# An early zero store to the output tensor, issued by ScalarE among the first loads, in a one-core decode kernel

## The chip, the core and the metric

The kernel runs on one core of a Trainium2 chip. The time is device time in microseconds of one execution. The profile is one further look at one execution; its span is about 1.8 us shorter than the timed figure, and times in views count from the start of the span.

Engines are named as in the profile: PE is the matrix engine (PEld its weight loads), DVE the vector engine, ACT ScalarE, POOL GpSimd and SP SyncE. A "q" after the name (ACTq, SPq) means an instruction handled by the engine's sequencer, such as the issue of a DMA. An issue only starts a transfer; the data land later. A completion semaphore is a counter that a DMA raises when its data have landed, so that others can wait for it.

## The reference, cut to what matters

```
g = sigmoid((x * gate_w).sum(-1))
a = attention(x @ wq, k_cache, v_cache) @ wo      # 32 heads, 4 KV heads, 65,536 keys, head size 128
b = gated MLP of x (w_in, layer norm, w_sp, b_sp, w_out)
return g * a + (1 - g) * b                        # 1 x 1 x 1024, bf16: 2 KB
```

One token is decoded. K and V are 67 MB each, the weights some 28 MB, all bf16, and all of it is read once. The result is 2 KB, so everything about the output is tiny beside the reads.

## The kernel before

The parts that matter are the first loads, the pool of four 32 KB-per-partition buffers that holds every big load, and the tail.

```python
# first loads: four small ones from ScalarE, four big ones from SyncE
nc.scalar.dma_start(out=xg8[:, 0, :], in_=A_x.rearrange(...))       # 8 rows x 256 B
nc.scalar.dma_start(out=xg8[:, 1, :], in_=gate_w.rearrange(...))
nc.scalar.dma_start(out=wb[:, 0:1], in_=B_w_sp)                     # one element
nc.scalar.dma_start(out=wb[:, 1:2], in_=B_b_sp.unsqueeze(0))        # one element
win_t = [load(win_view[:, i * KH:(i + 1) * KH, :], (KH, F), "win_t") for i in range(2)]   # SyncE
wq_t = [load(wq_view[:, i * KH:(i + 1) * KH, :], (KH, HD), "wq_t") for i in range(2)]
# ... constants by GpSimd and DVE, MLP, query; then 32 loads of K and V of 4 MB each ...
# tail: the last weights come in pieces of 16, 8, 4, 2, 1, 1 (4096 KB down to 256 KB)
for split in WO_SPLIT:
    # ... nc.sync.dma_start of a piece, then project() it into out_ps ...
out_sb = const.tile([P, NO], BF16, name="out_sb")
nc.scalar.copy(out=out_sb[:], in_=out_ps[:])
nc.scalar.dma_start(out=out.rearrange("o t (q n) -> (o t q) n", n=NO), in_=out_sb[::B, :])
```

The build puts in the semaphores. Each DMA gets one of eight completion semaphores, in turn, over all DMAs of SyncE and ScalarE together. A DMA that comes round to a semaphore waits until that semaphore's earlier DMA has landed.

Of the kernel before, what the change touches and what calls it, by code (L numbers as in the profile page):

```python
# [8 lines left out]
BF16 = mybir.dt.bfloat16  # L9
# [5 lines left out]
P = 128  # L15
CT = 128
NKV = 4
B = 32
NB = P // B
# [8 lines left out]
def kernel(  # L28
# [15 lines left out]
    nc = tc.nc  # L44

    _, _, D = A_x.shape
# [19 lines left out]
    const = ctx.enter_context(tc.tile_pool(name="const", bufs=1))  # L66
# [43 lines left out]
    def load_kv(src, g, j, name):  # L110
# [8 lines left out]
    wb = const.tile([1, 2], BF16, name="wb")  # L119
    nc.scalar.dma_start(out=wb[:, 0:1], in_=B_w_sp)  # L120
    nc.scalar.dma_start(out=wb[:, 1:2], in_=B_b_sp.unsqueeze(0))

    KH = KC // 2
    win_view = B_w_in.rearrange("(p c) n -> p c n", c=KC)
# [10 lines left out]
    erow = const.tile([KC, KC, P // KC], FP32, name="erow")  # L135
    nc.gpsimd.iota(erow[:], pattern=[[1, KC], [0, P // KC]], base=0, channel_multiplier=0,
                   allow_small_or_imprecise_dtypes=True)
    ones_f = const.tile([P, P], FP32, name="ones_f")
    nc.gpsimd.memset(ones_f[:], 1.0)
    wt = [big.tile([P, VC, BP, NB, VC, REP], BF16, name=f"wt{i}") for i in range(2)]  # L140
# [31 lines left out]
    for t in range(2):  # L172
        nc.vector.tensor_tensor(
            out=xm[:, t], in0=xb_ps[:, t * P:(t + 1) * P].rearrange("p (i c) -> p c i", c=KC),
# [51 lines left out]
    for hf in range(2):  # L226
        nc.vector.tensor_tensor(  # L227
            out=zm[:, hf], in0=z_ps[:, hf * HN:hf * HN + ZN].rearrange("p (j c) -> p j c", c=FC),
# [3 lines left out]
                            in_=zm.rearrange("p h j c -> p h c j"), axis=AX.X, op=ALU.add)  # L232
# [44 lines left out]
    for k in range(NHB):  # L277
        xs = slice(k * NX // NHB, (k + 1) * NX // NHB)
        nc.vector.tensor_tensor(  # L279
            out=qm[:, xs], in0=q_ps[:, k * HN:(k + 1) * HN].rearrange("p (x j e) -> p x j e",  # L280
                                                                   j=B, e=2),
# [6 lines left out]
        out=q4[:], in0=q1[:].rearrange("p x e -> p (x e)").unsqueeze(1).to_broadcast(  # L288
            [P, NB, NX * 2]),
# [7 lines left out]
    for g in range(G):  # L297
        k, t0 = g * T2 // NB, g * T2 % NB
        nc.vector.tensor_copy(out=qs[:, g].rearrange("p b (t h) -> p b t h", t=T2),
                              in_=qv[:, k, t0:t0 + T2].rearrange("p t h b -> p b t h"))  # L300
# [107 lines left out]
    NO = D // NB  # L408
# [35 lines left out]
    for split in WO_SPLIT:  # L444
        t = kv.tile([P, CT * P], BF16, name="wo_t", tag="kv")
        t = t[:].rearrange("p (c n) -> p c n", n=D)
        b = c0
        for n in split:
            nc.sync.dma_start(out=t[:, c0 - b:c0 - b + n, :], in_=wo_view[:, c0:c0 + n, :])  # L449
            project(t[:, c0 - b:c0 - b + n, :], n, oa, c0, last=(c0 + n == OC))  # L450
            c0 += n
    out_sb = const.tile([P, NO], BF16, name="out_sb")
    nc.scalar.copy(out=out_sb[:], in_=out_ps[:])  # L453
    nc.scalar.dma_start(out=out.rearrange("o t (q n) -> (o t q) n", n=NO), in_=out_sb[::B, :])

    last = {}
    for ins in list(nc.cur_bb.bb.instructions):
# [36 lines left out]
```

## Time and profile before

Three runs before the prediction: 385.80, 385.75 and 385.86 us.

| | before |
|---|---|
| DMA queue of SyncE | 98.5% of 16 engines' span, 422 GB/s |
| PE, DVE, ACT busy | 63%, 57%, 10% |
| first big packets (packet records) | 1.74 us |
| last weights landed | 380.64 us |
| end of the span | 383.92 us |

The first view below is the page: its DMA row in 40 slices of 9.6 us (tenths of busy time), the queue of SyncE, and the chain of waits by engine.

```profile
DMA  8999999999999999999999999999999999999995
q1 hardware_dynamic: 6192, 162.01, 98.5%
DMA 60%; DVE 20%; PE 11%; issue 5%; ACT 2%; SPq 1%; DVEq 0%; ACTq 0%
```

The stream of loads is full from the second slice on. DVE's and PE's shares of the chain lie beside it.

The timeline (start, duration, engine, line and operation) at the start of the kernel before:

```profile
0.74 0.61 ACTq L117 DMA_DIRECT2D xg<-in_A_x_dram  x1
1.39 0.29 ACTq L118 DMA_DIRECT2D xg<-in_gate_w_dram  x1
2.00 0.27 ACTq L121 DMA_DIRECT2D wb<-in_B_b_sp_dram  x1
2.31 1.28 ACT L190 ACT_TABLE_LOAD   x1 [2.31 <-issue]
7.64 0.37 PE L169 MATMUL xb_ps<-xg,spread 8*128 8x256 bf16 x1 [7.64 <-DMA xg<-in_gate_w_dram]
...
15.54 0.33 SPq L107 DMA_DIRECT2D kn<-in_A_k_cache_dram  x1
```

The first issue on ScalarE took 0.61 us, the three after it 0.27 to 0.29. The end of the chain of waits, and then the timeline of the last store:

```profile
349.05 31.60 DMA wo_t<-in_A_wo_dram
...
380.69 0.32 PE out_ps L414 x4
```

```profile
381.02 0.37 ACT L453 CAST out_sb<-out_ps 128x256 bf16<-128x256 f32 x1 [47.61 <-PE out_ps L414]
381.43 0.61 ACTq L454 DMA_DIRECT2D out_dram<-out_sb  x1
```

### The profile page before, as it was taken

What the parts mean: (1) busy time and instruction counts of PE and PEld (TensorE: products, weight loads), DVE (VectorE), ACT (ScalarE), POOL (GpSimd) and SP (SyncE); (2) the same over time, 40 slices, a digit from 0 to 9 for tenths busy, and PEclk for the clock granted to TensorE, in tenths of its full rate; (3) what the DMA queues carried; (4) which work ended last, traced back from release to release, by engine and by line L of the source; (5) the groups of instructions that cost most, each with busy time, mean ns of one, the idle gap of its engine ahead of it and who ended that gap; (6) DMA issues with size and microseconds to landing.
All of it is one profiled execution on the core that took longest, in us unless ns stands there. A gap on an engine that the chain in (4) does not pass through costs nothing.

```text
span 383.9 us, 2650 instructions
## 1 busy us (share of the span) xinstructions
PE 242.3 (63%) x1372; PEld 59.3 (15%) x796; DVE 218.5 (57%) x211; ACT 39.6 (10%) x55; POOL 4.4 (1%) x10
## 2 busy tenths in 40 slices
PE   0433447976449948466699393774993937685553
PEld 0110001111202201011121020121220201121122
DVE  5141478988497563658975545679754546730040
ACT  1010001100511101014011010140110101400000
POOL 4000000000000000000000000000000000000000
PEclk9996559889659989686599797865997869888868
DMA  8999999999999999999999999999999999999995
GB/s 335 430 437 437 435 434 430 423 431 426 428 427 437 435 430 437 427 434 430 423 432 427 437 437 422 430 434 437 427 425 427 437 438 427 425 430 431 434 411 203
DMA packets 6248, 162.18 MB, mean 422 GB/s; under 512 B 728, under 2 KB 732, under 8 KB 1116
## 3 DMA queue, kind: packets, MB, share of 16 engines
q1 hardware_dynamic: 6192, 162.01, 98.5%
q8 instruction: 8, 0.13, 0.1%
q14 instruction: 4, 0.03, 0.0%
q10 hardware_dynamic: 44, 0.01, 0.0%
HBM read 162.01 MB, written 0.00 MB: 422 GB/s over the span
## 4 chain that ended last, share of the span: by engine, by line
DMA 60%; DVE 20%; PE 11%; issue 5%; ACT 2%; SPq 1%; DVEq 0%; ACTq 0%
DMA kn<-in_A_k_cache_dram 47%; DVE kt L320 16%; DMA wo_t<-in_A_wo_dram 8%; PE s_ps L326 8%; DMA win_t<-in_B_w_in_dram 5%; DVE pt L362 2%; PE o_ps L372 2%; ACT sc L337 1%; PE z_ps L213 1%; ACT sc L359 1%; DVE mx L341 1%; DVE o_sb L387 0%; SPq L449 0%; ACT L359 0%; PE nb_ps L352 0%
## 5 line engine op out<-in xcount | busy, mean ns | idle before, releaser
L326 PE MATMUL s_ps<-kt,wt 128*128 128x512 bf16 x512 | 142.3, 437 | 67.9 <-DVE kt L320 67.3
L320 DVE STREAM_TRANSPOSE kt<-kn 128x2048 int32<-128x2048 int32 x64 | 143.3, 2284 | 63.5 <-DMA kn<-in_A_k_cache_dram 63.4
L372 PE MATMUL o_ps<-vt,pt 128*64 128x512 bf16 x512 | 69.2, 432 | 8.8 <-DMA vt<-in_A_v_cache_dram 8.8
L326 PEld LDWEIGHTS <-wt 128*128 128x128 bf16 x256 | 27.6, 108 | 184.0 <-issue 122.9
L337 ACT CAST sc<-s_ps 128x1024 bf16<-128x1024 f32 x16 | 16.2, 1013 | 253.8 <-PE s_ps L326 253.8
L372 PEld LDWEIGHTS <-pt 128*64 128x64 bf16 x256 | 17.2, 124 | 57.9 <-issue 56.4
L362 DVE STREAM_TRANSPOSE pt<-sc 128x1024 bf16<-128x1024 bf16 x16 | 18.6, 1218 | 6.8 <-ACT sc L359 6.8
L383 DVE TENSOR_TENSOR om<-o_ps,own 128x1024 f32<-128x1024 f32 x4 | 4.8, 1205 | 26.8 <-PE o_ps L372 26.8
L359 ACT ACTIVATE sc<-sc,nb 128x1024 bf16<-128x1024 bf16 x16 | 18.2, 1139 | 10.2 <-DVE nb L355 10.2
L322 DVE TENSOR_REDUCE mx<-sc 128x1 f32<-128x1024 bf16 x12 | 14.3, 1192 | 4.4 <-ACT sc L337 4.4
L341 DVE TENSOR_REDUCE mx<-sc 128x1 f32<-128x1024 bf16 x4 | 4.9, 1220 | 12.3 <-ACT sc L337 12.3
L213 PE MATMUL q_ps<-wq_t,xT 128*32 128x512 bf16 x64 | 7.2, 630 | 7.3 <-DMA wq_t<-in_A_wq_dram 7.3
L393 PE MATMUL om_ps<-o_sb,hsel 128*32 128x128 f32 x8 | 2.4, 398 | 13.6 <-DVE o_sb L387 13.6
L213 PE MATMUL z_ps<-win_t,xT 128*32 128x448 bf16 x64 | 6.4, 577 | 4.9 <-DMA win_t<-in_B_w_in_dram 4.9
L414 PE MATMUL out_ps<-wo_t,oa 128*32 128x256 bf16 x128 | 6.3, 346 | 4.6 <-DMA wo_t<-in_A_wo_dram 3.2
L279 DVE TENSOR_TENSOR rowt<-q_ps,own_b 128x512 f32<-128x512 f32 x2 | 1.3, 686 | 12.4 <-PE q_ps L213 12.4
L345 PE MATMUL mt_ps<-ident_f,m 128*1 128x128 f32 x4 | 1.4, 346 | 10.2 <-DVE m L343 10.2
L387 DVE TENSOR_REDUCE o_sb<-om 128x128 f32<-128x1024 f32 x4 | 7.5, 1871 | 0.1
L227 DVE TENSOR_TENSOR rowt<-z_ps,own_b 128x448 f32<-128x448 f32 x2 | 1.2, 620 | 9.6 <-PE z_ps L213 9.6
L213 PEld LDWEIGHTS <-xT 128*32 128x32 bf16 x64 | 3.0, 140 | 20.3 <-issue 20.3
L453 ACT CAST out_sb<-out_ps 128x256 bf16<-128x256 f32 x1 | 0.4, 372 | 47.6 <-PE out_ps L414 47.6
L414 PEld LDWEIGHTS <-oa 128*32 128x32 bf16 x128 | 4.2, 119 | 6.9 <-issue 4.2
(88 smaller groups left out, 57.9 us busy)
## 6 DMA issues: line engine op xcount, KB each, us to landing
kn<-in_A_k_cache_dram SPq DMA_DIRECT2D x16, 4096.0 KB, 26.5
vt<-in_A_v_cache_dram SPq DMA_DIRECT2D x16, 4096.0 KB, 32.9
wq_t<-in_A_wq_dram SPq DMA_DIRECT2D x2, 4096.0 KB, 28.4
win_t<-in_B_w_in_dram SPq DMA_DIRECT2D x2, 3584.0 KB, 15.1
wo_t<-in_A_wo_dram SPq DMA_DIRECT2D x1, 4096.0 KB, 27.2
wout_t<-in_B_w_out_dram SPq DMA_DIRECT2D x1, 3584.0 KB
wo_t<-in_A_wo_dram SPq DMA_DIRECT2D x1, 2048.0 KB
wo_t<-in_A_wo_dram SPq DMA_DIRECT2D x1, 1024.0 KB
```

The costliest lines, as they stand in the source:

```text
L213: ins = nc.tensor.matmul(ps[t * B:(t + 1) * B, k * HN:k * HN + n], lhsT=xT[:, i * KH + c:i * KH + c + 1].to_broadcast([P, B]), rhs=w[:, c, ...
L320: nc.vector.transpose(out=kt[:].bitcast(I32), in_=kb[:, v * n:(v + 1) * n])
L322: nc.vector.reduce_max(**late.pop())
L326: ins = nc.tensor.matmul(s_ps[:, k * HN:(k + 1) * HN], lhsT=wt[g % 2][:, v, b].rearrange("p a v h -> p (a v h)"), rhs=kx[:, b // 2, b % 2, ...
L337: nc.scalar.copy(out=sct[g, j][:], in_=s_ps[:])
L341: nc.vector.reduce_max(**late.pop())
L359: nc.scalar.activation(out=sct[g, j][:], in_=sct[g, j][:], func=ACT.Exp, scale=SCALE, bias=nb[:, 0:1], accum_out=lss[g][:, j:j + 1])
L362: nc.vector.transpose(out=ptt[g, j][:].rearrange("p c x -> p (c x)"), in_=sct[g, j][:])
L372: ins = nc.tensor.matmul(o_ps[g][hs, e, :], lhsT=ptt[g, j][:, 2 * u:2 * u + 2, :].rearrange("p c x -> p (c x)"), rhs=vx[:, 2 * u + e], sta ...
L383: nc.vector.tensor_tensor(out=om8[:], in0=o_ps[g][:].rearrange("p e (v d) -> p (e v) d", d=DH), in1=own_8[:].unsqueeze(2).to_broadcast([P, ...
L387: nc.vector.tensor_reduce(out=o_sb[:], in_=om8[:].rearrange("p x d -> p d x"), axis=AX.X, op=ALU.add)
L414: nc.tensor.matmul(out_ps[t * B:(t + 1) * B, :], lhsT=vec[:, c0 + c:c0 + c + 1].to_broadcast([P, B]), rhs=w[:, c, t * NO:(t + 1) * NO], st ...
```

## The change

The zero store touches the output once, early. It can have been meant to take some first-use cost of the output path (an address entry, a cold write) away from the exposed last store. The result is overwritten at the end, so the kernel stays correct.

```diff
     nc.scalar.dma_start(out=wb[:, 1:2], in_=B_b_sp.unsqueeze(0))
+    out_view = out.rearrange("o t (q n) -> (o t q) n", q=NB)
+    out_sb = const.tile([P, D // NB], BF16, name="out_sb")
 ...
+    nc.gpsimd.memset(out_sb[:], 0.0)
+    nc.scalar.dma_start(out=out_view, in_=out_sb[::B, :])
     ones_f = const.tile([P, P], FP32, name="ones_f")
     nc.gpsimd.memset(ones_f[:], 1.0)
 ...
-    out_sb = const.tile([P, NO], BF16, name="out_sb")
     nc.scalar.copy(out=out_sb[:], in_=out_ps[:])
-    nc.scalar.dma_start(out=out.rearrange("o t (q n) -> (o t q) n", n=NO), in_=out_sb[::B, :])
+    nc.scalar.dma_start(out=out_view, in_=out_sb[::B, :])
```

## The prediction

> **What bounds the kernel.** The stream of loads. The DMA table gives the SyncE queue 98.5% of 16 engines' span, 422 GB/s for 162 MB; in the 40 slices DMA stands at 9 tenths in all but the first and last. No compute engine is over 63%. The chain that ended last is 60% DMA, and its DVE and PE pieces lie beside a full DMA queue. So a small change counts only at the start, if it starved the load queue, and in the tail after the last load.
>
> **What the change adds.**
> 1. A GpSimd memset of 128x256 bf16 ahead of two others. The 128x128 f32 memset beside it took 0.20 us, so the GpSimd work behind it and the DVE setup held up beside that (two instructions of 3.3 us, to 5.1 us) move by about 0.2 us. PE's first matmul waits for the small ScalarE loads until 7.6 us: hidden.
> 2. A fifth ScalarE DMA, after four loads (issued 0.74 to 2.27 us, taking 0.61, 0.29, 0.27, 0.27). The table load behind it slips by 0.3 to 0.6 us; it ended at 3.6, and ScalarE's first work is at 12.4: hidden. Its four 512-byte rows stand behind the loads on the ScalarE rings, so they delay none. The Trainium skill (DMA: Bandwidth & Descriptors, "Queues, rings and completion order") says a DMA engine takes queues in turn by packets; the packet records agree: the last small loads come 1.1 us apart between 28 KB packets. The zeros should land at 12 to 14 us (estimate); nobody waits for them.
> 3. The last copy and last store must follow the zero store, done 370 us before: at most one more satisfied wait, 0.02 to 0.05 us by such waits in the trace.
>
> 2 KB written against 162 MB read is nothing. Even 1 us lost at the start is free: the four big loads already queued hold the DMA engines for about 35 us (15.7 MB at 430 GB/s, estimate), and the next is queued at 15.5.
>
> **What it could remove.** Only the tail is exposed: last weights land 380.64, copy 381.02 to 381.39, store issued 381.43 to 382.04, its packets 383.13 to 383.23, closing barrier to 383.9. If the aim is to warm the output's path, its reach is small: the packets take 0.1 us, so no slow first write is to be saved. The issue took 0.61 us, as did ScalarE's first DMA, against 0.27 to 0.29 for the next three. If the extra 0.33 us belongs to a first use of the output (its address entry, the store direction), the early store pays it and the end saves 0.3 us. If it is the price of a ScalarE queue that has not issued for a while, nothing is saved. I hold the second likelier (2 in 3): each later load was the first use of its own tensor, at 0.27 to 0.29. The 1.1 us from issue to packets should stay; SyncE's loads show the same.
>
> **Sum.** Minus 0.3 us with one chance in three, otherwise zero to plus 0.05: 385.7 us. Three runs before lie within 0.11 us.
>
> **What would show each step.** The early store's issue at 2.3 us, 0.6 long in the first theory, 0.3 in the second; the last issue 0.3 or 0.6. First matmul still at 7.6, first K load queued at 15.5, mean 422 GB/s, last weights landing at 380.6. HBM written 4096 bytes instead of 2048.
>
> **What would make it wrong.** A store among the loads that slows the stream by more than its bytes; a shifted memory layout; completion semaphores, handed round among DMAs, making a load wait for another transfer than before; a tail changed by something in the barrier that the profile doesn't name.

## More of the kernel before

The order of the first DMAs, read from the built programs (the zero store marked *):

```
semaphore        0     1       2        3      4      5       6       7       0 (waits)   1 (waits)
before           A_x   win[0]  gate_w   w_sp   b_sp   win[1]  wq[0]   wq[1]   K 0         K 1
changed          A_x   win[0]  gate_w   w_sp   b_sp   store*  win[1]  wq[0]   wq[1]       K 0
```

The trace's packet records put the four 512-byte packets of the last store, with their completion writes, at 382.67 to 382.77 us. SyncE's closing wait for them goes on at 383.11.

## The result

| | median, us | runs | range |
|---|---|---|---|
| before | 385.77 | 4 | 385.62 to 385.86 |
| changed | 385.87 | 4 | 385.68 to 385.88 |

The ratio is 1.0002, with a 95% interval of 0.9984 to 1.0019. Ratios here are the mean time of one kernel's fast runs over that of the other's of the same rounds, so not quite the ratio of the medians. The time is the same.

The page of the changed kernel, the same three rows:

```profile
DMA  8999999999999999999999999999999999999994
q1 hardware_dynamic: 6192, 162.01, 98.4%
DMA 67%; DVE 20%; issue 6%; PE 5%; ACT 1%; SPq 1%; DVEq 0%; ACTq 0%
```

The stream is as full as before. (The chain's 60 and 67% differ in its middle, where DVE and PE work lies beside a full queue; both chains begin and end alike.) The start of the changed kernel, in its timeline:

```profile
1.31 0.30 POOL L140 MEMSET out_sb<- 128x256 bf16 x1
2.01 0.27 ACTq L121 DMA_DIRECT2D wb<-in_B_b_sp_dram  x1
2.32 0.61 ACTq L141 DMA_DIRECT2D out_dram<-out_sb  x1
2.96 1.28 ACT L194 ACT_TABLE_LOAD   x1 [2.96 <-issue]
7.68 0.37 PE L173 MATMUL xb_ps<-xg,spread 8*128 8x256 bf16 x1 [7.68 <-DMA xg<-in_gate_w_dram]
...
15.38 0.33 SPq L107 DMA_DIRECT2D kn<-in_A_k_cache_dram  x1
```

The early store's issue took 0.61 us, directly behind an issue of 0.27. The table load slipped by 0.65 us. The first matmul moved from 7.64 to 7.68, and the first K load is queued at 15.38, 0.16 us earlier than before. The end of the chain and the last store:

```profile
349.88 30.78 DMA wo_t<-in_A_wo_dram
...
380.69 0.43 PE out_ps L418 x4
```

```profile
381.15 0.37 ACT L456 CAST out_sb<-out_ps 128x256 bf16<-128x256 f32 x1 [47.93 <-PE out_ps L418]
381.55 0.55 ACTq L457 DMA_DIRECT2D out_dram<-out_sb  x1
```

The last weights landed at 380.65, as before. The last issue took 0.55 us, not 0.61, and not 0.3. So neither of the two readings of the 0.61 us in the prediction fits: a first use would have given 0.61 and 0.3, an idle queue 0.3 and 0.61. That was the first thing to settle. The second came from the view of what SyncE's queue waited for (total us, times, longest), which has a line in the changed kernel that it did not have before:

```profile
SPq L107 <- DMA xg<-in_A_x_dram: 0.3, 1, 0.3
```

The fourth big load now waits for A_x, because the zero store moved every later DMA on by one completion semaphore (the table above). It waits 0.3 us, with three big loads queued, and nothing comes of it. The prediction had named this as a way to be wrong; the experiments ask how near it was.

### The profile page after: what moved, and what is told of

It reads as the page before. It is cut to its first block, busy times and chain, and to the rows that moved or that the text cites. A ratio compares the mean times of both kernels' runs of the same rounds, so it can differ in the third digit from the quotient of the medians.

```text
span 384.1 us, 2653 instructions
## 1 busy us (share of the span) xinstructions
PE 235.3 (61%) x1372; PEld 58.0 (15%) x796; DVE 218.6 (57%) x211; ACT 39.6 (10%) x55; POOL 4.6 (1%) x11
## 4 chain that ended last, share of the span: by engine, by line
DMA 67%; DVE 20%; issue 6%; PE 5%; ACT 1%; SPq 1%; DVEq 0%; ACTq 0%
DMA kn<-in_A_k_cache_dram 54%; DVE kt L324 17%; DMA wo_t<-in_A_wo_dram 8%; DMA win_t<-in_B_w_in_dram 5%; PE o_ps L376 2%; PE s_ps L330 1%; DVE pt L366 1%; PE z_ps L217 1%; ACT sc L341 1%; DVE o_sb L391 0%; SPq L453 0%; DVE mx L345 0%; DVE om L387 0%; DVE mx L326 0%; PE om_ps L397 0%
## 5 line engine op out<-in xcount | busy, mean ns | idle before, releaser
L330 PE MATMUL s_ps<-kt,wt 128*128 128x512 bf16 x512 | 136.1, 419 | 75.6 <-DVE kt L324 75.5
L330 PEld LDWEIGHTS <-wt 128*128 128x128 bf16 x256 | 26.7, 104 | 186.1 <-issue 121.2
L366 DVE STREAM_TRANSPOSE pt<-sc 128x1024 bf16<-128x1024 bf16 x16 | 18.6, 1217 | 6.8 <-ACT sc L363 6.8
L345 DVE TENSOR_REDUCE mx<-sc 128x1 f32<-128x1024 bf16 x4 | 4.9, 1220 | 12.1 <-ACT sc L341 12.1
L283 DVE TENSOR_TENSOR rowt<-q_ps,own_b 128x512 f32<-128x512 f32 x2 | 1.3, 686 | 12.1 <-PE q_ps L217 12.1
```

Of the source, the lines that this page charges most:

```text
L330: ins = nc.tensor.matmul(s_ps[:, k * HN:(k + 1) * HN], lhsT=wt[g % 2][:, v, b].rearrange("p a v h -> p (a v h)"), rhs=kx[:, b // 2, b % 2, ...
L345: nc.vector.reduce_max(**late.pop())
L366: nc.vector.transpose(out=ptt[g, j][:].rearrange("p c x -> p (c x)"), in_=sct[g, j][:])
```

## The experiments

Eleven kernels ran; all gave the reference's result. Times are medians, with the kernel before beside them.

| run | us | before | ratio, 95% interval |
|---|---|---|---|
| e1_probe | 386.05 (1 run) | 385.76 | |
| e2_late_store | 385.75 (1 run) | 385.76 | |
| e3_late_load | 385.81 (1 run) | 385.76 | |
| e4_sync_store | 385.70 | 385.76 | 0.9997 (0.9983 to 1.0011) |
| e5_slow_start | 385.95 | 385.82 | 1.0002 (0.9986 to 1.0019) |
| e6_two_last | 387.51 | 385.82 | 1.0043 (1.0028 to 1.0058) |
| e7_four_early | 388.58 | 385.84 | 1.0073 (1.0060 to 1.0085) |
| e8_four_later | 386.09 | 385.84 | 1.0006 (0.9994 to 1.0019) |
| e9_after_again | 385.88 | 385.84 | 1.0001 (0.9987 to 1.0014) |
| e10_three_early | 385.95 | 385.79 | 1.0004 (0.9990 to 1.0018) |
| e11_one_fewer | 385.72 | 385.81 | 0.9996 (0.9982 to 1.0010) |

### What does the issue of a store cost? (e1 to e4)

The theory after the result: every store issue is dear, about twice a load's, whatever went before it. Rivals: a change between loads and stores costs, the first use costs, the shape costs, or an idle queue costs.

```diff
# e1_probe, on the changed kernel (gate_w is also loaded before A_x); h is 64 columns, 128 B
-    nc.scalar.dma_start(out=out_view, in_=out_sb[::B, :])
+    nc.scalar.dma_start(out=bx[:, 0, :], in_=bx_view)                          # L1
+    nc.scalar.dma_start(out=out_view[:, 0:h], in_=out_sb[::B, 0:h])            # S1
+    nc.scalar.dma_start(out=out_view[:, h:2 * h], in_=out_sb[::B, h:2 * h])    # S2
+    nc.scalar.dma_start(out=bx[:, 1, :], in_=bx_view)                          # L2
+    nc.scalar.dma_start(out=bx[:, 2, :], in_=bx_view)                          # L3
+    nc.scalar.dma_start(out=out_view[:, 2 * h:], in_=out_sb[::B, 2 * h:])      # S3
```

> In place of the one early zero store, ScalarE issues in this order: gate_w load, A_x load (swapped), two 1-element loads, load of 4 rows x 512 B of B_x (L1), store of 4 rows x 128 B (S1), another such store (S2), the B_x load twice (L2, L3), a store of 4 rows x 256 B (S3); the last store of the result stays. Issue times by theory. Store price (every ScalarE store costs about 0.6): L1, L2, L3 about 0.28, S1, S2, S3 all about 0.6, last store 0.55 to 0.61. Switch (a change between loads and stores, or an address window that has to move, costs): S1 0.6, S2 0.28, L2 0.6, L3 0.28, S3 0.6. First use of the output: S1 0.6, S2 and S3 0.28. Shape (4 rows of 512 B cost more than 8 of 256 B): L1, L2, L3 0.6 too. First issue on the queue: gate_w, now first, 0.61 and A_x 0.28; if A_x itself was dear, the reverse. Time: 385.8 within 0.3, all of it hidden, by every theory.

The timeline of e1_probe, its issues on ScalarE:

```profile
0.74 0.61 ACTq L117 DMA_DIRECT2D xg<-in_gate_w_dram  x1
1.39 0.29 ACTq L118 DMA_DIRECT2D xg<-in_A_x_dram  x1
...
2.41 0.26 ACTq L144 DMA_DIRECT2D bx<-in_B_x_dram  x1
2.71 0.59 ACTq L145 DMA_DIRECT2D out_dram<-out_sb  x1
3.34 0.52 ACTq L146 DMA_DIRECT2D out_dram<-out_sb  x1
3.90 0.47 ACTq L147 DMA_DIRECT2D bx<-in_B_x_dram  x1
11.95 0.25 ACTq L148 DMA_DIRECT2D bx<-in_B_x_dram  x1
12.24 0.54 ACTq L149 DMA_DIRECT2D out_dram<-out_sb  x1
```

The stores took 0.59, 0.52 and 0.54 us; loads of four rows of 512 B took 0.26 and 0.25. That is the store price. It rules out the number and length of the rows as the cause, and a switch as the cause of what a store costs: S2 follows a store and would have cost 0.28. One load does not fit: L2, directly behind two stores, took 0.47, where the store price said 0.28 and the switch 0.6. It is the only load right behind a store in any run, so a switch may still cost a load some 0.2 us. Why is open. gate_w, now first on the queue, took 0.61 and A_x behind it 0.29, so ScalarE's first issue is dear, whichever tensor it is for.

e1_probe's time, 386.05 in its one run, lies within the expected 0.3 of 385.8, and the runs of the kernel before reach 386.03. In its profile the last weights landed at 380.92 instead of 380.64. With six extra early DMAs the second big load waits for a small one until about 9.5 us, and the other two for others until 11.75 us. These waits led to e7, but that they cost e1_probe its 0.28 us is not shown: the rates of its stretches are 344 GB/s from 8 to 10 us (373 before) and 418 or more after that, and by 30 us both kernels had moved the same 12.1 MB.

```diff
# e2_late_store, on the kernel before: a store of a scratch tile late in the program
+    nc.scalar.copy(out=late_sb[:, :OC], in_=oa[:])        # waits for the last head, about 372 us
+    nc.scalar.dma_start(out=out.rearrange("o t (q n) -> (o t q) n", n=NO), in_=late_sb[::B, :])
# e3_late_load: the same copy, then a load instead
+    nc.scalar.dma_start(out=bx[:], in_=B_x.rearrange("o t (q n) -> (o t q) n", n=NO))
```

> The kernel before, with a store to the output issued by ScalarE at about 371.5 us (its source waits for the last head's result), some 10 us before the last store overwrites it. Recent use of the queue, or recent use of the output: the last store's issue falls to about 0.3 and the span by 0.3. Store price: the last issue stays at 0.55 to 0.61, span and time as before (385.8 within 0.3). Packets of the late store start some 1 to 3 us after its issue, among the loads of wo, which should land no later than 380.6 plus 0.1.

> As the late store, but a load of 4 rows x 512 B of B_x issued by ScalarE at about 371.5 us. Recent use of the queue: last store's issue falls to 0.3. Recent use of the output alone, or store price: stays 0.55 to 0.61. The late load's own issue, after 370 us without one on ScalarE, tells what a queue out of use costs for a load: 0.28 if idleness costs nothing, 0.6 if it does.

The timelines of e2_late_store and then of e3_late_load, near the end:

```profile
372.61 0.60 ACTq L443 DMA_DIRECT2D out_dram<-late_sb  x1
...
381.45 0.52 ACTq L458 DMA_DIRECT2D out_dram<-out_sb  x1
```

```profile
372.36 0.26 ACTq L444 DMA_DIRECT2D bx<-in_B_x_dram  x1
...
381.41 0.61 ACTq L459 DMA_DIRECT2D out_dram<-out_sb  x1
```

A load after some 370 us without an issue cost 0.26: an idle queue costs nothing, against what the prediction thought likelier. Using the queue 9 us earlier with a load left the last store at 0.61. Using it with a store brought it to 0.52.

```diff
# e4_sync_store, on the kernel before
-    nc.scalar.dma_start(out=out.rearrange("o t (q n) -> (o t q) n", n=NO), in_=out_sb[::B, :])
+    nc.sync.dma_start(out=out.rearrange("o t (q n) -> (o t q) n", n=NO), in_=out_sb[::B, :])
```

> The kernel before, with the one last store issued by SyncE instead of ScalarE; SyncE's isolated load issues took 0.33. If the price is ScalarE's own: issue 0.33 instead of 0.6 plus one semaphore hop of 0.02 to 0.05, span and time 0.2 to 0.25 lower, 385.55. If it is the price of any store: issue about 0.6 on SyncE too, time the same within 0.1.

The last store of e4_sync_store in its timeline:

```profile
381.52 0.65 SPq L454 DMA_DIRECT2D out_dram<-out_sb  x1
```

SyncE's loads of K are issued in 0.33; its store took 0.65. The price belongs to stores, not to ScalarE. One rival was left untested: every store here reads four partitions that lie 32 apart (`[::B, :]`), while every small load writes partitions side by side. No run stores from neighbouring partitions, so the direction and this stride are not separated. Over all profiles, the first store of a program took 0.59 to 0.65 us (before, changed, e1, e2, e3, e4) and every later one that stands alone in a timeline 0.52 to 0.55 (changed, e1, e2, e5 to e11). So the early store does save something at the end: 0.06 us.

### Is the start hidden and the tail exposed? (e5, e6)

```diff
# e5_slow_start, on the changed kernel
-    for t in wt:
+    for t in wt * 3:
         nc.gpsimd.memset(t[:], 0.0)
# e6_two_last, on the changed kernel: the last line twice, the second waits for the first
     nc.scalar.dma_start(out=out_view, in_=out_sb[::B, :])
+    nc.scalar.dma_start(out=out_view, in_=out_sb[::B, :])
```

> The changed kernel with the two GpSimd clears of wt done three times: 4 more memsets of about 1.8 us, so GpSimd ends its setup some 7 us later and the DVE instructions beside it too. Hidden start (my claim): first matmul at about 12 to 14 instead of 7.7 us, first K load queued near 20 to 22 instead of 15.4, time 385.8 within 0.2, last weights at 380.65, because four big loads keep the stream going to about 36 us. Rival, the start is exposed: plus 4 to 7 us.

> The changed kernel with the last store issued twice in a row, the second waiting for the first. Exposed tail (my claim): the time grows by what one store takes from issue to landing, 1.8 us, 387.6 within 0.3; issues of both 0.52 to 0.55, unless recent use makes the second cheaper (0.3). Rival, part of the tail runs beside something else that ends later: less than 1.2.

The timeline of e5_slow_start at its start, and then that of e6_two_last at its end:

```profile
12.38 0.39 PE L173 MATMUL xb_ps<-xg,spread 8*128 8x256 bf16 x1 [12.38 <-DVE spread L162]
...
18.61 0.33 SPq L107 DMA_DIRECT2D kn<-in_A_k_cache_dram  x1
```

```profile
381.65 0.54 ACTq L457 DMA_DIRECT2D out_dram<-out_sb  x1
383.27 0.52 ACTq L458 DMA_DIRECT2D out_dram<-out_sb  x1
```

In e5_slow_start the first matmul ran at 12.38 us instead of 7.68 and the first K load was queued at 18.6 instead of 15.4; the time stayed the same (ratio 1.0002). The start is hidden, by several us at least. In e6_two_last the second store added 1.69 us (387.51 less 385.82), nearly the 1.8 expected; in its trace the two issues start 1.62 us apart, and one more closing wait (see e11) adds some 0.06. The tail is exposed in full, and the second issue took 0.52, so even a store right behind another is not at a load's price.

### How near is the semaphore trap? (e7, e8, e10, and e9 as the changed kernel again)

```diff
# e7_four_early, on the changed kernel; e10_three_early: three stores, of h, h and 2h columns
-    nc.scalar.dma_start(out=out_view, in_=out_sb[::B, :])
+    for i in range(4):
+        nc.scalar.dma_start(out=out_view[:, i * h:(i + 1) * h], in_=out_sb[::B, i * h:(i + 1) * h])
# e8_four_later: the same four stores, written just before build_w, after the query stage
```

The order of completion semaphores in the built programs (stores marked *):

```
semaphore   0     1       2        3      4      5       6       7       0        1        2        3
e10         A_x   win[0]  gate_w   w_sp   b_sp   store*  store*  store*  win[1]   wq[0]    wq[1]    K 0
e7          A_x   win[0]  gate_w   w_sp   b_sp   store*  store*  store*  store*   win[1]   wq[0]    wq[1]
e8          A_x   win[0]  gate_w   w_sp   b_sp   win[1]  wq[0]   store*  store*   wq[1]    store*   store*
```

In e7, win[1] comes round to the semaphore of win[0] and must wait until that has landed, with no other big load in the queue. In e10 it waits for A_x only, and wq[0] waits for win[0] while win[1] streams. In e8 the one that waits for win[0] is wq[1].

> The changed kernel with the zero store cut into four stores of 4 rows x 128 B at the same place. By the build's order the eight completion semaphores go round, so the second big SyncE load (win_t) must wait until the first has landed, at about 9.5 us, where the changed kernel's four big loads are issued by 3 us. Semaphore theory: the win_t pair's issue stretches to about 9, the DMA share falls below 0.9 between 8 and 10 us, the last weights land 0.2 to 0.4 later and the time is 386.05. Rival, stores are free and so are the waits: 385.8 with the last weights at 380.65. Second rival, each ScalarE store costs the stream: it would be slower by the same with the loads queued ahead, as in the next run. Store issues 0.6, then 0.52 to 0.55 three times; the last store 0.55.

> The same four zero stores, but written after the query stage, so that three big loads (11.5 MB, some 27 us of stream) are issued before any load has to wait for a semaphore; the fourth waits for the first load. Semaphore theory: win_t pair issued within 1 us, no gap, time 385.8, last weights 380.65. If the stores themselves slow the stream, 386.05 as in the run before.

> The changed kernel unaltered, for the size of its effect. The issue of the last store fell by 0.06 us in its profile; the fourth big load waited 0.3 us for a semaphore but with 11 MB queued ahead. Expected: 385.8, ratio between 0.9990 and 1.0010; last store issue 0.52 to 0.55; the A_x wait on SyncE again 0.2 to 0.4 and without effect.

> The changed kernel with the zero store cut into three at the same place (rows of 128, 128 and 256 B). By the build's order the second big load now waits only for A_x, which has landed by about 2.5 us, and the third waits for the first (12 us), with the second still queued. Semaphore theory: no gap in the stream, last weights 380.6 to 380.8, time 385.8 to 386.0, so the step of 2.7 us comes with the fourth store and not in proportion. If each early store cost the stream by itself: three quarters of it, about 387.9.

SyncE's waits until 16 us in e7_four_early (total us, times, longest), and the first and second big load in its timeline, merged into one line from the start of the first to the end of the second:

```profile
SPq L107 <- DMA win_t<-in_B_w_in_dram: 18.1, 2, 10.9
```

```profile
0.73 11.59 SPq L107 DMA_DIRECT2D win_t<-in_B_w_in_dram  x2
```

The table by stretches of the kernel before, then of e7_four_early (columns: stretch, length, busy time of PE, PEld, DVE, ACT, POOL with counts, granted clock, DMA share, GB/s):

```profile
8.00:10.00 2.00, 0.40 (x3) 0.43 (x2) 1.31 (x6) 0.00 (x0) 0.00 (x0) 1.00 0.87 373
10.00:12.00 2.00, 0.38 (x2) 0.29 (x3) 0.16 (x1) 0.00 (x0) 0.00 (x0) 1.00 1.00 430
12.00:14.00 2.00, 2.00 (x22) 0.73 (x14) 1.28 (x9) 0.17 (x1) 0.00 (x0) 1.00 0.96 416
```

```profile
8.00:10.00 2.00, 0.56 (x2) 0.50 (x2) 1.14 (x6) 0.00 (x0) 0.00 (x0) 1.00 0.88 373
10.00:12.00 2.00, 0.22 (x1) 0.22 (x2) 0.16 (x1) 0.00 (x0) 0.00 (x0) 1.00 0.41 173
12.00:14.00 2.00, 2.00 (x22) 0.73 (x14) 1.28 (x9) 0.17 (x1) 0.00 (x0) 1.00 0.86 229
```

The last weights in e7_four_early's chain:

```profile
352.33 31.14 DMA wo_t<-in_A_wo_dram
```

The second load was issued at 12.0 us, behind a wait of 10.9. The packet records show no packet of SyncE's queue at all for 1.31 us from 11.63. The last weights landed at 383.47, 2.83 later than before, and the time rose by 2.74 us. The dry 1.31 us is less than half of that; the stream also thins out before it and fills up slowly after it. From 10 to 14 us the two tables differ by 0.89 MB, which is 2.1 us of a stream of 422 GB/s (estimate); where the rest went was not traced. The mechanism was expected, the size was not: the expectation said 0.3, because it took 9.5 us in e1_probe for the landing of win[0], and that had been the landing of a small load (there win[1] waits for w_sp). win[0] has landed for SyncE at 12.0 us, and by then the queue has run dry; the next packet comes at 12.94.

The first two big loads of e10_three_early in its timeline, and the last weights in its chain:

```profile
0.74 1.75 SPq L107 DMA_DIRECT2D win_t<-in_B_w_in_dram  x2
```

```profile
350.55 30.04 DMA wo_t<-in_A_wo_dram
```

e10_three_early separates this from a price of each early store. Its second load is issued by 2.5 us, its packet records have no gap on that queue, its last weights landed at 380.59, and its time, ratio 1.0004, stands with the kernel before. Three early stores cost nothing that the rounds can tell, and the fourth 2.7 us: a step, not a slope. In e8_four_later the same four stores later in the program gave 1.0006; its last weights landed at 380.82, 0.2 us later. Whether those 0.2 us are the stores or scatter is left open.

e9_after_again, the changed kernel in five rounds: 1.0001. The last issue was 0.55 and the last weights landed at 380.66. The wait for A_x that was expected did not show at all: in this run A_x had landed by the time the fourth big load came up. So the new wait of the changed kernel sits at the edge of costing nothing even on its own queue.

### The closing waits (e11)

Setting the trace ends side by side showed where the saved 0.06 us goes. The table has the time from the end of the last store's last packet to the end of the span, from the trace's records.

| kernel | semaphore of the last store | waits that stand behind its own | closing, us |
|---|---|---|---|
| before, e4_sync_store | 7 | 0 | 1.15, 1.15 |
| changed, e9, e2, e3, e5 | 0 | 2 | 1.26 each |
| e1_probe | 5 | 2 | 1.28 |
| e6_two_last | 1 | 3 | 1.32 |
| e10, e7, e8 | 2, 3, 3 | 4 | 1.40, 1.42, 1.42 |

SyncE's closing row waits for semaphores (3,2), (4,1), (5,0), 6 and 7, in that order. Before, the last store has number 7 and stands last. In the changed kernel it has 0, and two more waits, both long satisfied, follow it. In the trace these instructions start 0.06 to 0.07 us apart. e3_late_load has no early store at all and the same 1.26, so it is the extra DMA and not the store.

```diff
# e11_one_fewer, on the changed kernel: one DMA fewer, so that the last store has semaphore 7 again
-WO_SPLIT = ((16,), (8, 4, 2, 1, 1))
+WO_SPLIT = ((16,), (12, 2, 1, 1))
```

> The changed kernel with the weights of wo fetched in pieces of 16, 12, 2, 1, 1 instead of 16, 8, 4, 2, 1, 1: one DMA fewer, so the last store gets the eighth completion semaphore again, as in the kernel before, whose wait stands last in SyncE's closing row of five waits. If each wait that stands behind the last store's costs at the end: from the last store packet to the end of the span 0.71 to 0.73 us, as before and in the SyncE-store run, instead of 0.82. The last store's issue stays at 0.55. Together the tail is about 0.05 shorter than before, 0.1 shorter than in the changed kernel; time 385.75 within 0.15, which the rounds can't tell from 385.8. If the closing depends on the number of DMAs or on the early store: 0.82 as in the changed kernel. Last weights at 380.65, if the piece of 12 is multiplied in time; if not, 0.1 to 0.3 later matmuls.

The closing took 1.15 us with the early store still there, as before (0.71 in the expectation's counting, which gives packet times 0.45 us later), so it depends on the semaphore's place. As a version that beats both, e11_one_fewer is not shown: its ratio is 0.9996 with 1 inside the interval, and its five runs spread from 385.50 to 386.12. Its profile is of the slowest of them, 386.12. There the larger piece of weights was not multiplied in time:

```profile
378.00 3.42 PE L418 MATMUL out_ps<-wo_t,oa 128*32 128x256 bf16 x64 [3.43 <-DMA wo_t<-in_A_wo_dram]
381.47 0.37 ACT L456 CAST out_sb<-out_ps 128x256 bf16<-128x256 f32 x1 [47.98 <-PE out_ps L418]
```

The 64 matmuls ran on to 381.4 without a pause for the last pieces, and the copy started at 381.47, 0.3 to 0.45 us later than in the two kernels. Whether the two runs of 385.50 and 385.55 did the same is not on record.

## Why the prediction was right

The time was right: 385.7 was predicted, 385.87 measured, the same. Point by point:

- **The bound, and the hidden start: right.** The last weights landed at 380.64 and 380.65. e5_slow_start shows that even several us of delay in the setup are free.
- **The zero store stands behind the loads and lands at 12 to 14 us: right.** The packet records show its first rows at 7.8 us, the last at 11.0, its last completion write at 12.1. The changed kernel's page counts 3 instructions more than before: the memset, the store and one wait. The trace counts 4096 bytes written instead of 2048.
- **The exposed tail: right.** e6_two_last added 1.69 us for one more store.
- **The two readings of the 0.61 us issue: both wrong,** the likelier one in kind (an idle queue costs nothing: 0.26 in e3_late_load), the other in size (0.06 us came back, not 0.33). The prediction put two chances in three on an idle queue and one on a first use of the output that would give 0.3 back. The step behind the idle queue, "each later load was the first use of its own tensor, at 0.27 to 0.29", was a fact about loads; the last DMA is a store. A store's issue takes 0.52 to 0.65 us on either engine. The first issue of the queue, 0.61, is a third thing that happened to have the same figure.
- **"Minus 0.3 us with one chance in three, otherwise zero to plus 0.05": the second branch held, by another sum.** From the start of the last copy to the end of the span is 2.90 us before and 2.94 in both profiles of the changed kernel: 0.06 saved at the issue, 0.11 added by the two closing waits. The kernel came out even, but not for the reason that the prediction held likelier; that the number was right here was in part luck. The rounds cannot resolve such an amount. In the profile of the changed kernel another 0.11 us lies in the last four matmuls (0.32 us before, 0.43 here, by the two chains); the granted clock from 380 to 381.2 us was 1.00 before and 0.50 there, and in e9_after_again, the same program, 1.00 with 0.32 again. That is scatter, not the change.
- **The packet times: wrong by 0.45 us,** as told above, and with them the "1.1 us from issue to packets"; it is 0.63 us (382.04 to 382.67), and 0.63 for the first SyncE load too (issue over at 1.11, first packet at 1.74). Nothing in the sum used them.
- **The semaphores as a danger: right in kind.** They moved by one place, the fourth big load got a new wait, and it was harmless because three big loads were queued. e7_four_early shows it at 2.7 us, and e10_three_early that two more stores would still have been free.

What stays open: what makes a store's issue dear (its direction or its partition stride), why L2 of e1_probe took 0.47, and the later landings of e1_probe (0.28 us) and e8_four_later (0.2 us).

## What to carry to other kernels

An early touch of the output has little to warm: the last store's issue fell by 0.06 us, and the tail gave it back. Before adding a small DMA among the first loads, look at which completion semaphore each big load then gets and what it must wait for; a harmless DMA can turn into a dry queue with no change in bytes. And in a tail of 3 us, do the sum by parts from the trace (landing, matmuls, copy, issue, packets, closing waits), because the timed runs scatter by more than the parts.

## What the Trainium skill lacked or had wrong

- DMA: Bandwidth & Descriptors gives no issue time by direction for this chip. Here an issue took 0.25 to 0.30 us for most small loads on ScalarE that follow another load (0.36 to 0.38 for the fourth load of e1_probe, e5_slow_start and e6_two_last), 0.33 for an isolated big load on SyncE, 0.52 to 0.65 for a store on either, and 0.59 to 0.62 for the first issue of ScalarE.
- The same page, "Anatomy of one DMA — SWDGE (gpsimd) path", puts most of a DMA's fixed 2 us in the write receipt of the target memory. That is said of the GpSimd path. For the ScalarE store of the kernel before, the issue starts at 381.43, its packets run from 382.67 to 382.77, and SyncE's wait goes on at 383.11: of 1.68 us, 1.24 lie before the first packet and 0.34 after the last.
- The same page, "Why a DMA increments its semaphore by 16 and not by 1", asks for one semaphore per DMA in flight. No page says what a small set of them, handed round by the build, does to the order of issue: a new wait of 0.3 us in the changed kernel, 10.9 us in e7_four_early, 2.7 us of time.
- No page gives the price of a satisfied wait in a closing row: 0.06 to 0.07 us each on SyncE.
- DMA: Bandwidth & Descriptors, "Queues, rings and completion order", on taking queues in turn by packets, agrees with the trace: the packets of the last two small loads and their completion writes come 1.1 us apart, at 7.85, 9.01, 10.08 and 11.14 us of the kernel before, beside packets of 28 KB that take some 1.07 us each. So does the 600 ns that "Latency and other measured facts" gives for the first byte on this path: from the end of the last store's issue to its first packet it was 0.63 us.
